# Weight narrowing handed out by single steps, four output banks in turn, and loads issued by need, in a fused retention and two-layer expert kernel

## The chip, the core and the metric

The kernel runs on one core of one Trainium2 chip. The metric is device time in microseconds of one execution, taken as the median of several. Engines are named as in the profile: PE (matmul), DVE, ACT, POOL and SP, which only issues DMAs.

## What is computed

```python
def _attn_ref(q, k, v):                      # B=4, H=8, S=768, D=64
    for t in range(S):                       # one decay rate gamma per head
        state = gamma * state + outer(k[:, :, t], v[:, :, t])
        y[:, :, t] = scale * q[:, :, t] @ state
    return y
...
x = attn_out as (3072 tokens, 512)
h = x @ moe_w_in                             # 512 -> 2048
g = where(h > 0, h, exp(min(h, 0)) - 1)
x = g @ moe_w_out                            # 2048 -> 512
h = x @ moe2_w_in
P = a[0] + a[1]*h + a[2]*h**2 + a[3]*h**3
Q = 1 + abs(b[0])*abs(h) + abs(b[1])*h**2
return (P / (Q + 1e-06)) @ moe2_w_out
```

## The kernel before

**Precision and weights.** The inputs are in float64. The big products are done as three fp32r matmuls each (high*high, high*low, low*high). Each of the four weight matrices is cut into 16 tiles, `wi` for the first product and `wo` for the second. A tile comes in as 512 KB of pairs of 32-bit words into one of three staging buffers `st` (`load_w`, L87), and is made into fp32 by one ACT instruction (`narrow_a`, L97, "the abs" below) and four DVE instructions (`narrow_b`, L110, L111, L112, L114, "the four steps"). Then `split_w` cuts it into a high part (ACT, L123) and a low part (POOL, L124). The list `todo` gives the order: weight 0 is `wi` tile 0, weight 1 is `wo` tile 0, weight 2 is `wi` tile 1, and so on; the first 32 belong to the first layer. Those of the second layer are narrowed later and stored to DRAM (`w2s`).

**Order.** Instructions of one engine run in the order in which the code writes them; engines wait for each other by semaphores alone. A DMA waits in SP's queue until its buffer is free, and all later DMAs of SP wait behind it.

**Up-front passes.** The sequence of 768 is cut into chunks of 128 tokens, six to a batch entry. Ten passes i = 0 to 9 do chunks 0 to 4, half of the heads in each pass (c = i // 2, g = i % 2). A pass does the scores (`sc`, L254), the chunk's addition to the state (`so`, L242 with the old state times a diagonal of decays `diag`, and L244), the masked scores `A` on DVE (L266), and, one pass later, the output (`at_out`: L275 and L278 into the same bank as `so`). Then ACT copies the state (L293) and the high part `xh` (L306), and DVE makes the low part `xl` (L307). Which of the PSUM banks `so` lies in is set in `at_in`. Weights 0 to 5 are narrowed in some of the passes: two steps behind `A`, two behind `xl`. Chunks are loaded in these passes too (`load_q`, `load_k`, 1 MB a chunk), and `scale_q`, `scale_k` on POOL multiply them by decays.

**Inner tiles.** After the passes one loop runs over (token block j, tile f) in the order of `seq`: six tiles of block 0, all 16 of block 1, the last ten of block 0, then blocks 2 to 5. An inner tile is: 12 matmuls of the first product (g1, into `h`), Relu and Exp on ACT (L598, L599), L603 on DVE, `gh` on ACT (L606), `gl` on POOL (L607), and 12 matmuls of the second product (g2, into the four banks `acc`), which are issued one tile later. In the first six tiles a further attention pass lies between g1 and g2 (`attn_a`, `attn_b`). `quota` says how many whole weights a tile narrows (0, 1 or 2): three steps before the Relu, the fourth behind L603, the split behind it, then the four steps of a second weight, and at the end the abs of the next.

```python
        run(steps[0:3])
...
        steps[3]()
...
        d1()
        run(steps[4:8])
        d2()
        if quota[it] and nabs[0] < nload[0]:
            abs_next()
```

After the first layer's last block the second layer runs over all blocks with weights that are ready.

Of the kernel before, what the change touches and what calls it, by code (L numbers as in the profile page):

```python
# [49 lines left out]
def retention_ffn_kernel(ctx: ExitStack, tc: tile.TileContext, qkT, kv, w1i, w1o, w2i, w2o, a_, b_, tab, out):  # L50
# [169 lines left out]
    def at_in(i, early=False):  # L220
# [7 lines left out]
        if early and i % 2:  # L228
# [236 lines left out]
    load_k(2)  # L465
    load_q(3)
    load_k(3)
    load_w(0, 0, 1)
# [17 lines left out]
    nc.gpsimd.tensor_copy(eye[:, 0:1], tri_t[:, 0:1])  # L486
    nc.gpsimd.tensor_tensor(out=eye[:, 1:C], in0=tri_t[:, 1:C], in1=tri_t[:, 0:C - 1], op=ALU.subtract)
    for p in range(NP):
        nc.gpsimd.tensor_scalar_mul(diag[:, p, :], eye, gc_t[:, p:p + 1])
# [29 lines left out]
    for i in range(10):  # L519
# [5 lines left out]
        at_mask(i, True)  # L525
        run(ops[0:2])
        if i:
            at_out(i - 1)
            run(at_state(i - 1))
            at_x(i - 1)  # L530
            if g == 0:
                load_q(c + 3)
                load_k(c + 3)
        run(ops[2:4])
        if ops:
            done()
            load_next()
            ops = []
        if i in (2, 4, 5, 6, 7, 8):
            ops, done = conv_next()  # L540
        if i == 9:
            abs_next()
# [3 lines left out]
    load_q(8)  # L546
    load_k(8)
    load_kr(2 * LATE)
    qp = atw.tile([128, 2, NP, C], F32R, tag="k0", name="qp", bufs=1)
    for e in range(2):  # L550
        nc.gpsimd.memset(qp[64 - 64 * e:128 - 64 * e, e].bitcast(F32), 0.0)
# [8 lines left out]

    half0 = 6
    seq = [(0, f) for f in range(half0)] + [(1, f) for f in range(KF)] + [(0, f) for f in range(half0, KF)]
    seq += [(j, f) for j in range(2, NB) for f in range(KF)]
    quota = [1, 1, 1, 2, 1, 2] + [1, 2, 1, 1, 2, 1, 1, 2] + [1] * 7 + [0] * 3 + [1] * 7 + [0]
    quota += [int(f % 2 == 1 or (j, f) == (2, 2)) for j in (2, 3, 4) for f in range(KF)] + [0] * KF
    assert sum(quota) == len(todo) - 6 and len(quota) == len(seq)
# [7 lines left out]
    for it, (j, f) in enumerate(seq):  # L574
# [7 lines left out]
        x1 = x2 = [none] * 4  # L582
        d1 = d2 = none
        if quota[it]:
            x1, d1 = conv_next()
        if quota[it] > 1:
            x2, d2 = conv_next()
        steps = x1 + x2
# [5 lines left out]
        run(steps[0:3])  # L594
# [4 lines left out]
        nc.scalar.activation(out=t, in_=t, func=ACTF.Exp, scale=-1.0)  # L599
        run(st)  # L600
# [7 lines left out]
        steps[3]()  # L608
        if it < half0 + 8:
            fill(3 if quota[it] < 2 else 2)  # L610
        else:
            fill(1)
        d1()
        run(steps[4:8])
        d2()
        if quota[it] and nabs[0] < nload[0]:
            abs_next()
# [16 lines left out]
        if it < half0 + 8:  # L634
            fill(3)
# [113 lines left out]
```

## Time and profile before

| what | value |
|---|---|
| median of 3 runs | 1204.96 us (1204.39 to 1205.35) |
| time of the profiled execution | 1204.38 us |
| its span, first to last instruction | 1202.6 us |
| PE busy in the span | 1181.9 us (98%) |
| DVE, ACT, POOL busy | 830.5, 689.8, 452.7 us |
| mean granted clock of PE | 0.996 |

The span is the stretch that the trace shows; some 1.8 us of the profiled execution's time lie around it. PE's busy time is 98% of the span, and the page's row of the 40 slices of PE falls below nine tenths in the first two slices and in the last alone. A matmul counts as busy from its issue to its modelled end.

### The profile page before, as it was taken

What the parts mean: (1) busy time and instruction counts of PE and PEld (TensorE: products, weight loads), DVE (VectorE), ACT (ScalarE), POOL (GpSimd) and SP (SyncE); (2) the same over time, 40 slices, a digit from 0 to 9 for tenths busy, and PEclk for the clock granted to TensorE, in tenths of its full rate; (3) what the DMA queues carried; (4) which work ended last, traced back from release to release, by engine and by line L of the source; (5) the groups of instructions that cost most, each with busy time, mean ns of one, the idle gap of its engine ahead of it and who ended that gap; (6) DMA issues with size and microseconds to landing.
All of it is one profiled execution on the core that took longest, in us unless ns stands there. A gap on an engine that the chain in (4) does not pass through costs nothing.

```text
span 1202.6 us, 15571 instructions
## 1 busy us (share of the span) xinstructions
PE 1181.9 (98%) x5684; PEld 993.6 (83%) x5684; DVE 830.5 (69%) x1228; ACT 689.8 (57%) x1214; POOL 452.7 (38%) x376
## 2 busy tenths in 40 slices
PE   8899999999999999999999999999999999999998
PEld 7787778888888888888888888888888888888887
DVE  4888775876666556665311598788888888888775
ACT  2445554444444444444455787777776767776765
POOL 6454554443333333322378533233223232232222
PEclk9999999999999999999999999999999999999999
DMA  9724331554224322422243300200100200200000
GB/s 260 222 86 153 107 111 68 171 171 167 88 88 141 126 89 91 151 89 75 88 123 107 113 10 1 62 10 1 62 10 1 70 1 1 70 1 1 35 1 35
DMA packets 57068, 97.81 MB, mean 81 GB/s; under 512 B 11680, under 2 KB 25120, under 8 KB 56992
## 3 DMA queue, kind: packets, MB, share of 16 engines
q1 hardware_dynamic: 56704, 96.49, 25.1%
q8 instruction: 44, 0.72, 0.2%
q10 hardware_dynamic: 288, 0.34, 0.1%
q14 instruction: 32, 0.26, 0.1%
HBM read 74.79 MB, written 22.02 MB: 81 GB/s over the span
## 4 chain that ended last, share of the span: by engine, by line
PE 89%; DVE 6%; ACT 2%; issue 1%; DMA 1%; POOL 0%; ACTq 0%; DVEq 0%
PE acc L341 41%; PE h L341 40%; PE so L278 3%; PE sc L341 2%; DVE wc L112 1%; DVE wc L111 1%; DVE wc L110 1%; PE so L244 1%; PE so L275 1%; DVE wc L114 1%; ACT wc L97 1%; DMA qT<-in_qkT_dram 1%; DVE t L603 1%; DVE xl L307 0%; ACT gh L606 0%
## 5 line engine op out<-in xcount | busy, mean ns | idle before, releaser
L341 PE MATMUL h<-xh,wi 128*128 128x512 f32 x1536 | 507.1, 391 | 0.0
L341 PEld LDWEIGHTS h<-xh,wi 128*128 128x128 f32 x1536 | 288.4, 188 | 58.9
L341 PE MATMUL h<-xl,wi 128*128 128x512 f32 x768 | 299.2, 390 | 0.0
L678 POOL TENSOR_TENSOR gl<-e,gh 128x512 fp32r<-128x512 f32 x96 | 124.7, 1299 | 349.6 <-ACT gh L677 214.4
L607 POOL TENSOR_TENSOR gl<-t,gh 128x512 fp32r<-128x512 f32 x96 | 124.2, 1293 | 320.8 <-ACT gh L606 293.8
L341 PE MATMUL acc<-gh,wo 128*128 128x512 f32 x768 | 196.1, 398 | 6.3 <-ACT gh L606 4.9
L341 PE MATMUL acc<-wo,gh 128*128 128x512 f32 x768 | 190.1, 389 | 0.0
L341 PEld LDWEIGHTS acc<-gh,wo 128*128 128x128 f32 x768 | 142.2, 189 | 36.3 <-ACT gh L606 6.2
L341 PEld LDWEIGHTS acc<-wo,gh 128*128 128x128 f32 x768 | 144.1, 188 | 29.9
L341 PEld LDWEIGHTS h<-xl,wi 128*128 128x128 f32 x768 | 144.4, 188 | 29.0
L603 DVE SCALAR_TENSOR_TENSOR t<-t,h 128x512 f32<-128x512 f32 x96 | 65.6, 683 | 128.0 <-ACT t L599 127.9
L598 ACT ACTIVATE t<-h 128x512 f32<-128x512 f32 x96 | 57.2, 595 | 148.4 <-PE h L341 148.0
L652 ACT ACTIVATE s<-h 128x512 f32<-128x512 f32 x96 | 57.4, 598 | 137.8 <-PE h L341 137.8
L606 ACT CAST gh<-t 128x512 fp32r<-128x512 f32 x96 | 59.7, 622 | 108.9 <-DVE t L603 108.9
L658 DVE SCALAR_TENSOR_TENSOR u<-s,b,u 128x512 f32<-128x512 f32 x96 | 71.9, 749 | 56.4 <-ACT u L653 55.8
L341 PE MATMUL acc<-wo,gl 128*128 128x512 f32 x384 | 103.1, 389 | 0.0
L341 PE MATMUL acc<-gl,wo 128*128 128x512 f32 x384 | 103.1, 390 | 0.0
L668 DVE SCALAR_TENSOR_TENSOR e<-e,ab,r 128x512 f32<-128x512 f32 x96 | 72.2, 752 | 32.2 <-ACT r L662 32.2
L669 DVE SCALAR_TENSOR_TENSOR u<-u,r 128x512 f32<-128x512 f32 x96 | 87.6, 913 | 0.0
L341 PEld LDWEIGHTS acc<-gl,wo 128*128 128x128 f32 x384 | 72.1, 188 | 15.7
L341 PEld LDWEIGHTS acc<-wo,gl 128*128 128x128 f32 x384 | 72.1, 188 | 15.0
L654 ACT ACTIVATE e<-h,ab 128x512 f32<-128x512 f32 x96 | 74.9, 780 | 0.0
(107 smaller groups left out, 1609.5 us busy)
## 6 DMA issues: line engine op xcount, KB each, us to landing
st<-in_w1i_dram SPq DMA_DIRECT2D x16, 512.0 KB, 3.6
st<-in_w1o_dram SPq DMA_DIRECT2D x16, 512.0 KB, 3.5
st<-in_w2i_dram SPq DMA_DIRECT2D x16, 512.0 KB, 4.7
st<-in_w2o_dram SPq DMA_DIRECT2D x16, 512.0 KB, 3.7
w2s<-wc SPq DMA_DIRECT2D x32, 256.0 KB, 2.1
wc<-w2s SPq DMA_DIRECT2D x32, 256.0 KB, 2.7
xs<-y SPq DMA_DIRECT2D x24, 256.0 KB, 3.6
qT<-in_qkT_dram SPq DMA_DIRECT2D x20, 256.0 KB, 3.9
```

The costliest lines, as they stand in the source:

```text
L278: nc.tensor.matmul(out=so[:, p, :], lhsT=vw[:, 2 * g + p, e:e + 2, :], rhs=A[:, 2 * p + e, :], start=(c % CB == 0 and e == 0), stop=(e == 1))
L341: nc.tensor.matmul(out=ps, lhsT=lh, rhs=rh, start=first and idx == 0, stop=last and idx == len(pairs) - 1)
L598: nc.scalar.activation(out=t, in_=h, func=ACTF.Relu, scale=-1.0)
L603: nc.vector.scalar_tensor_tensor(out=t, in0=t, scalar=-1.0, in1=h, op0=ALU.add, op1=ALU.max)
L606: nc.scalar.copy(gh, t)
L607: nc.gpsimd.tensor_tensor(out=gl, in0=t, in1=gh.bitcast(F32), op=ALU.subtract)
L652: nc.scalar.activation(out=s, in_=ps, func=ACTF.Square)
L654: nc.scalar.activation(out=e, in_=ps, func=ACTF.Identity, scale=ab[:, 3:4], bias=ab[:, 2:3])
L658: nc.vector.scalar_tensor_tensor(out=u, in0=s, scalar=b1, in1=u, op0=ALU.mult, op1=ALU.add)
L668: nc.vector.scalar_tensor_tensor(out=e, in0=e, scalar=ab[:, 0:1], in1=r, op0=ALU.add, op1=ALU.mult)
L669: nc.vector.scalar_tensor_tensor(out=u, in0=u, scalar=QC, in1=r, op0=ALU.add, op1=ALU.mult)
L678: nc.gpsimd.tensor_tensor(out=gl, in0=e, in1=gh.bitcast(F32), op=ALU.subtract)
```

## The change

It joins five edits.

1. In the up-front passes `so` takes four banks in turn (`acc3`, two buffers of `h`, one of `pst`); before, every odd pass took `acc3`.
2. The diagonal of decays is made by DVE (six small instructions) and no longer by POOL.
3. In the passes the abs of the next weight stands before the split of the present one, and weights are narrowed in passes 3, 4, 5, 6, 8, 9 instead of 3, 5, 6, 7, 8, 9.
4. Loads are reordered: weight 1 before chunk 3; chunk 6 two passes later, chunk 7 behind the first inner tile, chunk 8 and the zeroing of `qp` behind the third.
5. In the inner tiles `nops` gives single steps (five in most tiles) instead of whole weights. Three stand before the Relu, the rest behind L603 (L624 in the changed kernel). The split of a weight whose four steps are done stands behind the next Relu and Exp (`finish`), in block 1; in the other blocks also at the end of the tile's DVE work. The abs runs at most one weight ahead.

```diff
--- before.py
+++ after.py
@@ -225,7 +225,7 @@
             sc = psa.tile([128, 4, C], F32, tag=f"acc{i % 4}", name="sc")
         else:
             sc = pst.tile([128, 4, C], F32, tag="sc", name="sc")
-        if early and i % 2:
+        if early and i % 4 == 1:
             so = psa.tile([128, 4, C], F32, tag="acc3", name="so")
         elif early and i % 4:
             so = psh.tile([128, 4, C], F32, tag="h", name="so")
@@ -463,9 +463,9 @@
     load_w(0, 0, 0)
     load_q(2)
     load_k(2)
+    load_w(0, 0, 1)
     load_q(3)
     load_k(3)
-    load_w(0, 0, 1)
     load_w(0, 1, 0)
     ab = const.tile([128, 6], F32, name="ab")
     nc.sync.dma_start(out=ab[:, 0:4], in_=a_.rearrange("(o n) -> o n", o=1).to_broadcast([128, 4]))
@@ -483,10 +483,14 @@
     scale_k(0)
     scale_q(1, nc.gpsimd)
     eye = dg[:, 512:512 + C]
-    nc.gpsimd.tensor_copy(eye[:, 0:1], tri_t[:, 0:1])
-    nc.gpsimd.tensor_tensor(out=eye[:, 1:C], in0=tri_t[:, 1:C], in1=tri_t[:, 0:C - 1], op=ALU.subtract)
-    for p in range(NP):
-        nc.gpsimd.tensor_scalar_mul(diag[:, p, :], eye, gc_t[:, p:p + 1])
+
+    def decay_diag(p):
+        nc.vector.tensor_scalar_mul(diag[:, p, :], eye, gc_t[:, p:p + 1])
+
+    nc.vector.tensor_copy(eye[:, 0:1], tri_t[:, 0:1])
+    nc.vector.tensor_tensor(out=eye[:, 1:C], in0=tri_t[:, 1:C], in1=tri_t[:, 0:C - 1], op=ALU.subtract)
+    decay_diag(0)
+    decay_diag(1)
     todo = [(ph, f, e) for ph in range(2) for f in range(KF) for e in range(2)]
     nload, nabs, nconv = [3], [0], [0]
 
@@ -523,32 +527,29 @@
             scale_k(c + 2)
         at_in(i, True)
         at_mask(i, True)
+        if i == 0:
+            decay_diag(2)
+            decay_diag(3)
         run(ops[0:2])
         if i:
             at_out(i - 1)
             run(at_state(i - 1))
             at_x(i - 1)
-            if g == 0:
-                load_q(c + 3)
-                load_k(c + 3)
+            if i in (2, 4, 8):
+                load_q(min(c + 3, 6))
+                load_k(min(c + 3, 6))
         run(ops[2:4])
+        if i in (3, 4, 5, 7, 8, 9):
+            abs_next()
         if ops:
             done()
             load_next()
             ops = []
-        if i in (2, 4, 5, 6, 7, 8):
+        if i in (2, 3, 4, 5, 7, 8):
             ops, done = conv_next()
-        if i == 9:
-            abs_next()
     at_out(9)
     run(at_state(9))
     at_x(9)
-    load_q(8)
-    load_k(8)
-    load_kr(2 * LATE)
-    qp = atw.tile([128, 2, NP, C], F32R, tag="k0", name="qp", bufs=1)
-    for e in range(2):
-        nc.gpsimd.memset(qp[64 - 64 * e:128 - 64 * e, e].bitcast(F32), 0.0)
     nc.scalar.activation(out=b1, in_=ab[:, 5:6], func=ACTF.Abs)
     nx[0] = 9
     attn_b()
@@ -558,12 +559,37 @@
         nc.sync.dma_start(out=c, in_=w2s[f][e])
         W[1, f, e, "c"] = c
 
+    qp = atw.tile([128, 2, NP, C], F32R, tag="k0", name="qp", bufs=1)
+    def first_late():
+
+        load_q(LATE)
+        load_k(LATE)
+        load_kr(2 * LATE)
+        for e in range(2):
+            nc.gpsimd.memset(qp[64 - 64 * e:128 - 64 * e, e].bitcast(F32), 0.0)
+
     half0 = 6
     seq = [(0, f) for f in range(half0)] + [(1, f) for f in range(KF)] + [(0, f) for f in range(half0, KF)]
     seq += [(j, f) for j in range(2, NB) for f in range(KF)]
-    quota = [1, 1, 1, 2, 1, 2] + [1, 2, 1, 1, 2, 1, 1, 2] + [1] * 7 + [0] * 3 + [1] * 7 + [0]
-    quota += [int(f % 2 == 1 or (j, f) == (2, 2)) for j in (2, 3, 4) for f in range(KF)] + [0] * KF
-    assert sum(quota) == len(todo) - 6 and len(quota) == len(seq)
+    nops = [5, 5, 5, 5, 6, 6] + [5] * 12 + [4] * 3 + [0] * 3 + [4] * 7 + [0]
+    nops += [4 * int(f % 2 == 1 or (j, f) == (2, 2)) for j in (2, 3, 4) for f in range(KF)] + [0] * KF
+    assert sum(nops) == 4 * (len(todo) - 6) and len(nops) == len(seq)
+    stream, ends = [], []
+
+    def narrow(n):
+
+        for _ in range(n):
+            if not stream:
+                ops, done = conv_next()
+                stream.extend(ops)
+                ends.append([done])
+            stream.pop(0)()
+            if not stream:
+                ends[-1].append(True)
+
+    def finish():
+        while ends and len(ends[0]) > 1:
+            ends.pop(0)[0]()
 
     def fill(n):
 
@@ -579,24 +605,19 @@
         at_b = both or (1 < j < NB - 1 and f % 2 == 1)
         h = psh.tile([128, 512], F32, tag="h", name="h")
         g1(h, f, xh, xl)
-        x1 = x2 = [none] * 4
-        d1 = d2 = none
-        if quota[it]:
-            x1, d1 = conv_next()
-        if quota[it] > 1:
-            x2, d2 = conv_next()
-        steps = x1 + x2
+        n = nops[it]
         st = []
         if at_a:
             low = prep(nx[0] + 1)
             at_mask(nx[0])
             low()
-        run(steps[0:3])
+        narrow(min(n, 3))
         if at_a:
             st = attn_a()
         t = tmp("t", "t")
         nc.scalar.activation(out=t, in_=h, func=ACTF.Relu, scale=-1.0)
         nc.scalar.activation(out=t, in_=t, func=ACTF.Exp, scale=-1.0)
+        finish()
         run(st)
         if at_a:
             at_x(nx[0])
@@ -605,16 +626,16 @@
         gl = gp.tile([128, 512], F32R, tag="gl", name="gl")
         nc.scalar.copy(gh, t)
         nc.gpsimd.tensor_tensor(out=gl, in0=t, in1=gh.bitcast(F32), op=ALU.subtract)
-        steps[3]()
-        if it < half0 + 8:
-            fill(3 if quota[it] < 2 else 2)
+        if j == 1:
+            if n and nabs[0] < min(nload[0], nconv[0] + 1):
+                abs_next()
+            narrow(max(n - 3, 0))
         else:
-            fill(1)
-        d1()
-        run(steps[4:8])
-        d2()
-        if quota[it] and nabs[0] < nload[0]:
-            abs_next()
+            narrow(max(n - 3, 0))
+            if n and nabs[0] < min(nload[0], nconv[0] + 1):
+                abs_next()
+            finish()
+        fill((3 if it < half0 + 8 else 1) - (1 if stream else 0))
         if last:
             split_w(1, f, 0)
             if f + 1 < KF:
@@ -632,9 +653,14 @@
                 split_w(1, f - 1, 1)
             load_c(f, 1)
         if it < half0 + 8:
-            fill(3)
+            fill(2 if stream else 3)
         elif not last and it not in (19, 20, 21, 30, 31, 47, 63, 79):
             fill(2)
+        if it == 0:
+            load_q(7)
+            load_k(7)
+        if it == 2:
+            first_late()
         if (j, f) == (0, KF - 1):
             load_ya()
         if j == NB - 2 and f == KF - 1:
```

What the change moves on the engines is shown at three places. The first is ACT in passes 2 to 4 (`St` is the state, `xh` the high part of the block's input, L97 the abs, L123 the split). Before:

```order
L306 CAST xh<-so 128x2x128
L123 CAST wi_324<-wc 128x512
L293 COPY St<-so 64x2x64 x2
L306 CAST xh<-so 128x2x128
L97 ACTIVATE wc<-st 128x512
L293 COPY St<-so 64x2x64 x2
L306 CAST xh<-so 128x2x128
L123 CAST wo_387<-wc 128x512
L97 ACTIVATE wc<-st 128x512
```

and changed:

```order
L306 CAST xh<-so 128x2x128
L97 ACTIVATE wc<-st 128x512
L123 CAST wi_326<-wc 128x512
L293 COPY St<-so 64x2x64 x2
L306 CAST xh<-so 128x2x128
L97 ACTIVATE wc<-st 128x512
L123 CAST wo_366<-wc 128x512
L293 COPY St<-so 64x2x64 x2
L306 CAST xh<-so 128x2x128
L97 ACTIVATE wc<-st 128x512
```

Each pass has an abs now, and the abs stands ahead of the split, which waits for DVE's fourth step. An abs that waits for its load holds the copies of the state behind it.

The second is SP's queue behind chunk 5 (rows of `v_139`), with the loads of weights 4 to 7 (L87) and of chunk 6 (`li_145` to `lo_154`). Before:

```order
L172 DMA v_139<-in_kv_dram 128x3x128
L173 DMA v_139<-in_kv_dram 128x2x64
L87 DMA st<-in_w1i_dram 128x1024
L158 DMA li_145<-in_qkT_dram 128x512
L163 DMA li_145<-in_kv_dram 128x512
L167 DMA li_156<-in_qkT_dram 64x512 x2
L172 DMA lo_154<-in_kv_dram 128x3x128
L173 DMA lo_154<-in_kv_dram 128x2x64
L87 DMA st<-in_w1o_dram 128x1024
L87 DMA st<-in_w1i_dram 128x1024
L158 DMA lo_146<-in_qkT_dram 128x512
```

and changed:

```order
L172 DMA v_139<-in_kv_dram 128x3x128
L173 DMA v_139<-in_kv_dram 128x2x64
L87 DMA st<-in_w1i_dram 128x1024
L87 DMA st<-in_w1o_dram 128x1024
L87 DMA st<-in_w1i_dram 128x1024
L158 DMA li_145<-in_qkT_dram 128x512
L163 DMA li_145<-in_kv_dram 128x512
L167 DMA li_156<-in_qkT_dram 64x512 x2
L172 DMA lo_154<-in_kv_dram 128x3x128
L173 DMA lo_154<-in_kv_dram 128x2x64
L87 DMA st<-in_w1o_dram 128x1024
L87 DMA st<-in_w1i_dram 128x1024
```

Weights 4, 5 and 6 follow chunk 5 one behind the other; before, chunk 6 stood between weights 4 and 5.

The third is DVE in three tiles of block 1 (L603 and L624 are the same instruction of an inner tile). Before, one weight, one weight and the first of two:

```order
L603 SCALAR_TENSOR_TENSOR t<-t,h 128x512
L114 SCALAR_TENSOR_TENSOR wc<-st,wc 128x512
L110 TENSOR_SCALAR wc<-wc 128x512
L111 TENSOR_SCALAR wc<-wc 128x512
L112 SCALAR_TENSOR_TENSOR wc<-st,wc 128x512
L114 SCALAR_TENSOR_TENSOR wc<-st,wc 128x512
L110 TENSOR_SCALAR wc<-wc 128x512
L111 TENSOR_SCALAR wc<-wc 128x512
L112 SCALAR_TENSOR_TENSOR wc<-st,wc 128x512
```

and changed:

```order
L624 SCALAR_TENSOR_TENSOR t<-t,h 128x512
L110 TENSOR_SCALAR wc<-wc 128x512
L111 TENSOR_SCALAR wc<-wc 128x512
L112 SCALAR_TENSOR_TENSOR wc<-st,wc 128x512
L114 SCALAR_TENSOR_TENSOR wc<-st,wc 128x512
L110 TENSOR_SCALAR wc<-wc 128x512
L624 SCALAR_TENSOR_TENSOR t<-t,h 128x512
L111 TENSOR_SCALAR wc<-wc 128x512
L112 SCALAR_TENSOR_TENSOR wc<-st,wc 128x512
L114 SCALAR_TENSOR_TENSOR wc<-st,wc 128x512
L110 TENSOR_SCALAR wc<-wc 128x512
L111 TENSOR_SCALAR wc<-wc 128x512
L624 SCALAR_TENSOR_TENSOR t<-t,h 128x512
```

Between one L603 and the next stood four or eight steps; now five stand there, and a weight's four steps lie across the boundary of tiles.

## Rows read from the trace of the kernel before

**Rows 1.** Stages (us): busy time (instructions) of PE, PEld, DVE, ACT, POOL; PE clock; DMA share, GB/s

```profile
6.40:48.94 42.54, 35.50 (x272) 34.29 (x273) 27.56 (x48) 14.22 (x38) 21.19 (x21) 0.92 0.94 267
48.94:103.08 54.14, 52.18 (x298) 45.14 (x296) 42.71 (x56) 27.99 (x59) 29.73 (x24) 1.00 0.35 116
103.08:166.43 63.35, 57.01 (x241) 45.75 (x240) 50.88 (x67) 34.01 (x59) 31.25 (x23) 0.97 0.37 129
166.43:1203.00 1036.57, 1032.32 (x4867) 864.91 (x4865) 706.53 (x1050) 612.26 (x1058) 365.68 (x295) 1.00 0.21 68
```

**Rows 2.** Waits of PE from 0 to 166 us: total us, times, longest us

```profile
PE acc L341 <- ACT gh L606: 4.9, 3, 2.5
PE so L242 <- DVE xl L307: 4.2, 3, 1.9
PE so L244 <- POOL lo L183: 2.1, 1, 2.1
PE so L278 <- DVE A L266: 2.0, 3, 1.1
...
PE acc L341 <- ACT li L398: 1.4, 1, 1.4
```

**Rows 3.** Timeline of DVE, end of the passes: start, duration, instruction, idle before it

```profile
40.64 0.69 DVE L114 SCALAR_TENSOR_TENSOR wc<-st,wc 128x512 int32<-128x512 int32 x1
...
46.98 1.03 DVE L110 TENSOR_SCALAR wc<-wc 128x512 f32<-128x512 f32 x1 [0.66 <-ACT wc L97]
...
49.44 0.69 DVE L114 SCALAR_TENSOR_TENSOR wc<-st,wc 128x512 int32<-128x512 int32 x1
...
52.53 0.68 DVE L266 TENSOR_TENSOR A<-sc,mask 128x512 f32<-128x512 f32 x1
53.13 2.68 DVE L110 TENSOR_SCALAR wc<-wc 128x512 f32<-128x512 f32 x1
55.84 0.43 DVE L111 TENSOR_SCALAR wc<-wc 128x512 int32<-128x512 int32 x1
```

**Rows 4.** Timeline of ACT at the end of the passes

```profile
50.16 0.62 ACT L123 CAST wo<-wc 128x512 fp32r<-128x512 f32 x1 [2.20 <-DVE wc L114]
50.69 0.66 ACT L97 ACTIVATE wc<-st 128x512 f32<-128x512 f32 x1
51.25 0.52 ACT L293 COPY St<-so 64x128 f32<-64x128 f32 x2
```

**Rows 5.** Timeline of SP's queue: issue of weight 3's load and chunk 5's last

```profile
25.52 0.41 SPq L87 DMA_DIRECT2D st<-in_w1o_dram  x1
...
29.80 0.43 SPq L173 DMA_DIRECT2D v<-in_kv_dram  x1
```

**Rows 6.** DMA issues in 25.5:25.6 and 29.79:29.83 us: KB, us from issue to landing

```profile
st<-in_w1o_dram SPq DMA_DIRECT2D x1, 512.0 KB, 5.4
...
v<-in_kv_dram SPq DMA_DIRECT2D x1, 64.0 KB, 4.8
```

**Rows 7.** Chain that ended last, from 160 us: start, us, what

```profile
169.31 2.72 PE acc L341 x12
172.03 2.72 PE h L341 x12
```

**Rows 8.** Timeline of PE: the longest wait in block 1

```profile
139.01 1.22 PE L341 MATMUL acc<-gh,wo 128*128 128x512 f32 x2 [2.49 <-ACT gh L606]
```

**Rows 9.** Groups of DVE instructions, 103:166 us: count, busy us, mean ns, idle before

```profile
L111 DVE TENSOR_SCALAR wc<-wc 128x512 int32<-128x512 int32 x14 | 15.7, 1120 | 0.5
L112 DVE SCALAR_TENSOR_TENSOR wc<-st,wc 128x512 int32<-128x512 int32 x13 | 11.9, 916 | 0.4
L110 DVE TENSOR_SCALAR wc<-wc 128x512 f32<-128x512 f32 x14 | 9.0, 643 | 12.6 <-ACT wc L97 12.6
L114 DVE SCALAR_TENSOR_TENSOR wc<-st,wc 128x512 int32<-128x512 int32 x13 | 8.9, 686 | 0.1
L603 DVE SCALAR_TENSOR_TENSOR t<-t,h 128x512 f32<-128x512 f32 x10 | 6.8, 681 | 0.0
```

**Rows 10.** Timeline of POOL and DVE in block 1

```profile
126.32 1.48 POOL L124 TENSOR_TENSOR wi<-wc,wi 128x512 fp32r<-128x512 f32 x1
...
126.69 1.40 DVE L111 TENSOR_SCALAR wc<-wc 128x512 int32<-128x512 int32 x1
```

**Rows 11.** Timeline of SP's queue in block 1: two loads that share a buffer

```profile
110.91 0.33 SPq L87 DMA_DIRECT2D st<-in_w1i_dram  x1
...
124.95 0.33 SPq L87 DMA_DIRECT2D st<-in_w1o_dram  x1
```

## The prediction

> **What bounds the kernel now.** I read the table of stages first [rows 1]. The reader is to see that from 166.43 us to the end PE is busy for 1032.32 of 1036.57 us, at full clock; what is missing lies behind the last matmul. Nothing that the change does there can matter as long as it adds no wait: the order on all engines is the same as before from the end of block 1 on. In the three stages ahead of it PE is idle for 42.54 - 35.50 = 7.0, 54.14 - 52.18 = 2.0 and 63.35 - 57.01 = 6.3 us, and in the first and third its clock is below full (0.92 and 0.97). So the whole change is about some 20 us at the start.
>
> The second view is the waits of PE in that stretch [rows 2]: 4.9 us for `gh` and 1.4 us for copies of the accumulators in block 1, 4.2 us for `xl`, which holds the bank that the next odd pass wants, 2.1 us for the scaled chunk 1, 2.0 us for `A`. Behind all of them stands the narrowing of weights. In the passes DVE's last step of a weight starts every 4.40 us (at 40.64 and 49.44, with one between) [rows 3], while PE could do a pass in less; in block 1 tiles with two weights make L603 late, then `gh`, then g2, by up to 2.49 us [rows 8].
>
> How long block 1 must take follows from the chain of work further on: 12 matmuls take 2.72 us, a tile 2 x 2.72 = 5.44 us [rows 7]. Ten tiles lie between 103.08 and 166.43, 54.4 us of work in 63.35 us: **8.95 us are lost there**, 6.3 in waits and the rest at a lower clock behind them (the clock of the stage is 0.97).
>
> **Block 1: single steps.** The same number of steps is done over the stage; what is new is how they lie. DVE's need per tile: as measured, with everything that holds them up inside their durations, the four steps take 0.643 + 1.120 + 0.916 + 0.686 = 3.37 us a weight, L603 0.68 [rows 9]. Five steps and one L603 make 1.25 x 3.37 + 0.68 = 4.89 us, less than PE's 5.44. A tile of two weights needed 7.4, and the waits for the abs came on top: 12.6 us in 14 weights, since it stood behind `gh` and the split [rows 9]. Now the abs runs a weight ahead in three tiles of four, and the split stands behind Exp. ACT per tile has Relu, Exp, `gh` and 1.25 of split and abs, some 3.4 us at the 0.6 or so that each takes [rows 4], so neither engine is full. `gh` is wanted by PE a whole tile, 5.44 us, after its `h` is done. I take all 8.95 us as won; the lower bound is worked out with the rivals.
>
> One row speaks against it. L111 takes 1.40 us when it meets a running POOL subtraction and 0.43 us otherwise, and it ends 0.29 us behind POOL's end (126.69 + 1.40 against 126.32 + 1.48) [rows 3, 10]. The Trainium skill ("SBUF — State Buffer", "Who interferes with whom") says the same as a rule: DVE and GpSimd share a port pair, and a DVE instruction in a 2-port mode or with two SBUF inputs waits for the whole of a GpSimd one. It speaks against this change, because a DVE that no longer idles behind the abs starts more of its steps while POOL runs. By that rule alone, with every step held that meets POOL, up to the 6.3 us of the first rival below would be given back.
>
> By the rows of before the holds cost 3.37 - 2.23 = 1.14 us a weight, where 2.23 is two steps at 0.43 and two at 0.69 (L110 unheld taken as long as L111). DVE keeps pace with PE up to (5.44 - 0.68) / 1.25 = 3.81 us a weight, that is holds of 1.58 us.
>
> **The passes.** Each of the removed waits (2.1 for chunk 1, behind the diagonal on POOL; 4.2 for `xl`, through the fourth bank) is hidden by what is late next: first the loads, then the narrowing. DMA moves 267 GB/s through the stage at a share of 0.94 [rows 1], so loads come no sooner. Weight 3's load stands in the same place of the stream as before and lands at 25.52 + 5.4 = 30.9 us [rows 5, 6]; its abs (0.66) ends at 31.6. In pass 6 its four steps (2.23) and `xl` (0.4), with one hold of about 1.0, end at 35.2; before, weight 3 ended at 40.64 + 0.69 = 41.3. That is 6.1 us ahead, because pass 4 has a weight now. Weight 4 follows chunk 5, which lands at 29.80 + 4.8 = 34.6; 512 KB at 267 GB/s are 2.0 us, so it lands at 36.6 and its abs ends at 37.2. Two weights follow at 4.40 - 0.66 = 3.74 us each (the abs no longer stands behind the split), 44.7, and with one further hold about 45.7; before, weight 5 ended at 50.13. What follows is a fixed chain: split, abs, state, `xh`, `xl`, then `A` of the tenth pass at 52.53, for which PE waits [rows 3, 4]; the abs leaves it (51.25 - 50.69 = 0.56 us). So the first inner tile gets its `A` 4.4 + 0.56 = 5.0 us sooner, with one hold fewer 6.0. I take 5.5. Bounds: 2.1 us if the last two weights take 4.40 + 1.0 us each (no wait saved, one hold more): 37.2 + 10.8 = 48.0 against 50.13. 10 us if narrowing holds nothing and PE goes by the landing of chunk 5: 34.6, a scaling on POOL of 1.5 as the subtraction takes [rows 10], some 30 small matmuls at 35.50 / 272 = 0.13 us [rows 1] and the first g1 of 2.72 us [rows 7] come to 42.7 against 52.53. A loss in this stage would need weight 3 to be narrowed later than before, and its load, which sets it, stands where it stood.
>
> The diagonal on DVE costs six instructions of 128 columns or fewer, below 1 us in all, at a place where DVE waits for the first scores; I cost it at nothing, and 1 us if POOL's scaling of chunk 0 holds it.
>
> **The six tiles of block 0.** They lose 2.0 us to waits now. The zeroing of `qp` no longer stands in front of L110 (2.68 us at 53.13 instead of 0.43 [rows 3]), but a fifth step, with an inline abs in front of it, now stands between L603 and the next `A`, and PE waits for `A`. With tiles of about 7.7 us DVE has room, apart from the first two. I take 0, between -1.5 and +1.5. Chunks 7 and 8 come later, but one to two tiles ahead of their scaling.
>
> **The sum.** 5.5 + 0 + 8.9 = 14.4 us off the profiled execution's 1204.4 gives **1190.0 us**. The profiled execution is 0.6 us below the median shown, so no correction is made.
>
> **Rivals.**
> - *POOL's holds fill DVE in block 1.* For: the row on L111 and the loss of the idle time that kept them apart. Against: 1.14 is well below 1.58. At 2.0 us of holds a weight, 4.23 us, a tile takes 1.25 x 4.23 + 0.68 = 5.97; 0.53 us over twelve tiles with five steps are 6.3 of the 8.9 given back: 1196.3.
> - *The passes stay where they were.* Every abs now stands ahead of the split and of the copies of the state, and DMA is full; a late landing holds ACT, hence the state, hence PE. Then only block 1 pays, with 2 us at most from the passes: about 1194.5.
> - *The passes open up to PE's own pace.* If fewer holds occur than I count, the stage ends 8 to 10 us sooner, and the tiles of block 0 lose nothing: 10 + 1 + 8.9, 1184.5.
> - *Slower: the three staging buffers become the bound of block 1.* Now a buffer comes round in 124.95 - 110.91 = 14.0 us [rows 11], paced by DVE. At 1.25 weights a tile it must come round in 3 x 5.44 / 1.25 = 13.1. Abs and steps have their slots once a tile, so a load that misses a slot costs up to 5.44 us. At 17.2 us a tile would take 17.2 / 3 x 1.25 = 7.17, 1.73 more than PE needs, 20.8 us over twelve tiles: 1204.4 + 20.8 - 8.9 - 5.5 = 1210.8. It decides for slower from about 16.4 us on (16.8 us lost). Against it: a load lands in some 5 us [rows 6], and the load is asked for behind the fourth step of the weight three places ahead, so that by my count of slots four microseconds or more are left.
>
> **How the numbers follow.** A measurement of this kernel tells about 0.2%, 2.4 us, from no change. Chances: my forecast 0.55, the holds 0.13, the passes unchanged 0.12, the passes opened 0.13, the staging buffers 0.04, and 0.03 for gains and losses that cancel. The range reaches from the opened passes (1184.5) to just beyond the holds with a little less from the passes as well (1197.0); the slower rival and a part of the unlikeliest mixtures are left out. Faster by over 0.2%: 0.93; within: 0.03; slower: 0.04.
>
> **What would show it.** In the profile after, PE's waits for `gh` in block 1 should be gone, and ten tiles there take 54 to 55 us at a clock of 1.00; L110 should no longer wait for L97 except for one tile in four. The waits of L242 for `xl` should be gone, and in their place PE waits for the state (L293) or for `A` in passes 6 to 9, while L97 waits for loads of weights 2 to 4. `A` of the tenth pass should start at about 47 us. From the end of block 1 on, the timeline should be the same, shifted. I am wrong if L111, L112 and L110 together take over 3.1 us a weight in block 1, if ACT waits for loads there, or if a new wait shows up behind 150 us.

## The result and the profile after

The changed kernel takes **1191.79 us** (median of four, 1190.54 to 1192.73) against 1205.15 (1204.39 to 1205.66) for the kernel before: a ratio of 0.9889, 95% interval 0.9872 to 0.9906. The forecast was 1190.0 in a range of 1184.5 to 1197.0. The profiled execution shown below, 1192.73 us, is the slowest of the four.

The stages of the changed kernel, cut at the same events as [rows 1] (columns as there):

```profile
6.75:46.11 39.36, 33.92 (x273) 32.81 (x273) 28.76 (x54) 14.71 (x39) 20.34 (x15) 0.96 0.95 270
46.11:100.01 53.90, 51.76 (x297) 44.97 (x296) 43.24 (x60) 28.30 (x59) 30.95 (x24) 1.00 0.41 134
100.01:154.43 54.42, 54.42 (x242) 45.06 (x241) 49.02 (x62) 33.26 (x58) 30.50 (x22) 1.00 0.39 135
154.43:1191.00 1036.57, 1032.59 (x4867) 864.82 (x4865) 711.22 (x1051) 612.43 (x1059) 367.97 (x296) 1.00 0.21 69
```

PE's waits in the whole execution, which answer to [rows 2]:

```profile
PE so L242 <- ACT St L293: 4.3, 2, 2.5
PE so L278 <- DVE A L266: 2.1, 2, 1.5
PE wps L477 <- DVE warm L434: 1.5, 1, 1.5
PE so L244 <- POOL n L183: 0.6, 1, 0.6
PE sc L254 <- POOL li L178: 0.4, 1, 0.4
```

In block 1 PE is busy for all of 54.42 us, at full clock, and no wait for `gh` is left; the last wait of PE in the whole execution ends before 57 us. From the end of the ten tiles to the last instruction the kernel takes 1036.5 us, before 1036.1. Measured from the first score matmul to the first g1, and from g1 to g1, the stages changed like this (the third stage of the views begins with the second tile of block 1, so its first tile is counted with block 0):

| us | before | after | saved |
|---|---|---|---|
| up-front passes | 42.50 | 39.30 | 3.20 |
| six tiles of block 0, first of block 1 | 54.13 | 53.90 | 0.23 |
| next ten tiles of block 1 | 63.35 | 54.40 | 8.95 |
| ahead of the first score and behind the ten tiles | 1042.59 | 1043.35 | -0.76 |

Block 1 gave all that was forecast, to the hundredth. In this execution the passes gave 3.2 where 5.5 were forecast. The DVE instructions from 100 to 155 us, answering to [rows 9]:

```profile
L114 DVE SCALAR_TENSOR_TENSOR wc<-st,wc 128x512 int32<-128x512 int32 x13 | 12.3, 950 | 0.3
L111 DVE TENSOR_SCALAR wc<-wc 128x512 int32<-128x512 int32 x13 | 11.6, 889 | 0.3
L112 DVE SCALAR_TENSOR_TENSOR wc<-st,wc 128x512 int32<-128x512 int32 x12 | 11.4, 950 | 0.3
L110 DVE TENSOR_SCALAR wc<-wc 128x512 f32<-128x512 f32 x13 | 10.5, 804 | 4.4 <-ACT wc L97 4.4
L624 DVE SCALAR_TENSOR_TENSOR t<-t,h 128x512 f32<-128x512 f32 x10 | 6.8, 680 | 0.0
```

The four steps take 0.950 + 0.889 + 0.950 + 0.804 = 3.59 us a weight, 1.36 of it holds (1.14 before). The holds did grow, as the row on L111 had warned, but stayed under the 1.58 at which DVE was to fall behind. The wait for the abs fell from 12.6 to 4.4 us, and that is nearly all of DVE's idle time: in the ten tiles DVE stood idle for 63.35 - 50.88 = 12.5 us before and 54.42 - 49.02 = 5.4 now.

The end of the passes on DVE, answering to [rows 3]: the last steps of weights 3, 4 and 5 (L114), the `xl` that stands in front of weight 4's last two steps, and the `A` for which PE waits:

```profile
34.92 0.69 DVE L114 SCALAR_TENSOR_TENSOR wc<-st,wc 128x512 int32<-128x512 int32 x1
...
41.67 0.42 DVE L307 TENSOR_TENSOR xl<-so,xh 128x256 fp32r<-128x256 f32 x1 [1.37 <-ACT xh L306]
42.02 0.68 DVE L112 SCALAR_TENSOR_TENSOR wc<-st,wc 128x512 int32<-128x512 int32 x1
42.73 0.69 DVE L114 SCALAR_TENSOR_TENSOR wc<-st,wc 128x512 int32<-128x512 int32 x1
...
46.74 0.69 DVE L114 SCALAR_TENSOR_TENSOR wc<-st,wc 128x512 int32<-128x512 int32 x1
...
49.27 0.68 DVE L266 TENSOR_TENSOR A<-sc,mask 128x512 f32<-128x512 f32 x1
```

And on ACT, where the abs (L97) of weight 3 (at 31.64) and of weight 4 (at 38.35) stand:

```profile
31.64 0.66 ACT L97 ACTIVATE wc<-st 128x512 f32<-128x512 f32 x1 [3.87 <-POOL n L183]
...
37.51 0.54 ACT L293 COPY St<-so 64x128 f32<-64x128 f32 x2 [1.25 <-PE so L278]
38.08 0.37 ACT L306 CAST xh<-so 128x256 fp32r<-128x256 f32 x1
38.35 0.69 ACT L97 ACTIVATE wc<-st 128x512 f32<-128x512 f32 x1
```

POOL's L183 was over long before 31.64; that abs waited for its load, which by its DMA record landed at 31.55. Weight 3 ended at 34.92 + 0.69 = 35.61 (35.2 forecast). Weight 4's load landed at 37.17, but its abs ended at 39.04 (37.2 forecast): the copies of the state and `xh` stand in front of it on ACT and waited for PE's L278. Then weight 4 took until 43.42 and weight 5 until 47.43, so 4.38 and 4.01 us. Together that is 8.39 us where 7.48, or 8.48 with one hold, were forecast: two of a weight's steps stand behind `xl`, which waits for `xh`, so a weight cannot be quicker than a pass. The first inner tile's `A` came at 49.27, 3.26 us sooner than in [rows 3], not 5.5.

### The profile page after: what moved, and what is told of

Its sections match the earlier page's. It is cut to its first block, busy times and chain, and to the rows that moved or that the text cites. A ratio compares the mean times of both kernels' runs of the same rounds, so it can differ in the third digit from the quotient of the medians.

```text
span 1190.9 us, 15583 instructions
## 1 busy us (share of the span) xinstructions
PE 1177.9 (99%) x5684; PEld 991.5 (83%) x5684; DVE 835.0 (70%) x1234; ACT 690.0 (58%) x1214; POOL 454.6 (38%) x370
## 4 chain that ended last, share of the span: by engine, by line
PE 93%; DVE 2%; DMA 2%; POOL 1%; issue 1%; ACT 1%; SPq 0%; POOLq 0%; ACTq 0%; DVEq 0%
PE acc L341 43%; PE h L341 42%; PE so L278 3%; PE sc L341 2%; PE so L244 1%; PE so L275 1%; DMA lo<-in_qkT_dram 1%; DMA st<-in_w1i_dram 0%; DMA k<-in_qkT_dram 0%; POOL gl L628 0%; PE sc L254 0%; DVE wc L112 0%; POOL wi L124 0%; DVE wc L111 0%; DVE wc L110 0%
## 5 line engine op out<-in xcount | busy, mean ns | idle before, releaser
L628 POOL TENSOR_TENSOR gl<-t,gh 128x512 fp32r<-128x512 f32 x96 | 128.9, 1343 | 274.2 <-ACT gh L627 266.2
L624 DVE SCALAR_TENSOR_TENSOR t<-t,h 128x512 f32<-128x512 f32 x96 | 65.5, 682 | 128.8 <-ACT t L619 128.8
L694 DVE SCALAR_TENSOR_TENSOR e<-e,ab,r 128x512 f32<-128x512 f32 x96 | 72.1, 752 | 32.5 <-ACT r L688 32.5
L112 DVE SCALAR_TENSOR_TENSOR wc<-st,wc 128x512 int32<-128x512 int32 x64 | 73.7, 1151 | 1.8
```

The costliest lines, as they stand in the source:

```text
L112: lambda: v.scalar_tensor_tensor(out=ci, in0=t[:, :, 1], scalar=-0x40000000, in1=ci, op0=ALU.bitwise_and, op1=ALU.bitwise_or),
L624: nc.vector.scalar_tensor_tensor(out=t, in0=t, scalar=-1.0, in1=h, op0=ALU.add, op1=ALU.max)
L628: nc.gpsimd.tensor_tensor(out=gl, in0=t, in1=gh.bitcast(F32), op=ALU.subtract)
L694: nc.vector.scalar_tensor_tensor(out=e, in0=e, scalar=ab[:, 0:1], in1=r, op0=ALU.add, op1=ALU.mult)
```

## The experiments

My theory: block 1 is worth 8.9 us and belongs to edit 5, the single steps, alone; the passes are worth some 3 to 5 us and end with narrowing and loads. Rivals: POOL's holds fill DVE as soon as it stops idling; parts of the change do nothing; the clock or the place of the abs explains what the passes missed.

**The two halves apart.** First the steps alone, edit 5, on the kernel before:

```diff
-    quota = [1, 1, 1, 2, 1, 2] + [1, 2, 1, 1, 2, 1, 1, 2] + [1] * 7 + [0] * 3 + [1] * 7 + [0]
+    nops = [5, 5, 5, 5, 6, 6] + [5] * 12 + [4] * 3 + [0] * 3 + [4] * 7 + [0]
...
-        run(steps[0:3])
+        narrow(min(n, 3))
```

> The kernel before with edit 5 alone (single steps in the inner tiles, abs ahead, split behind Exp). Theory: block 1 pays by itself, 8.9 us: about 1196.2 us, ten tiles of block 1 in 54.4 us, the passes as before (42.5 us). Rival: single steps only keep pace because the passes hand over weights earlier; then waits for gh stay in block 1 and the time is 1200 us or more.

Measured 1199.66 us (1196.68 to 1201.10), ratio 0.9954 (0.9941 to 0.9966). Its passes, block 0 and block 1:

```profile
6.76:51.62 44.86, 35.75 (x272) 34.39 (x273) 26.44 (x47) 14.21 (x38) 20.71 (x21) 0.92 0.94 261
51.62:106.44 54.82, 51.76 (x298) 44.98 (x296) 43.34 (x60) 28.83 (x60) 30.57 (x24) 1.00 0.35 111
106.44:160.84 54.40, 54.40 (x242) 45.05 (x240) 48.99 (x62) 33.28 (x58) 30.50 (x22) 1.00 0.41 136
```

Block 1 takes 54.40 us with this edit alone, and no wait for `gh` is left, so the rival fell. The 3.5 us that are missing to the expectation lie ahead of it: the passes took 2.4 us more than in [rows 1] with the same instructions in the same order, and loads landed later in them (by the DMA records weight 0 at 16.11 us against 15.11, weight 5 at 42.81 against 41.55), and a tile of block 0 waited 2.3 us for `A`. Only the fastest of its five executions came near the 1196.2.

Then everything but the steps, edits 1 to 4:

```diff
-    nops = [5, 5, 5, 5, 6, 6] + [5] * 12 + [4] * 3 + [0] * 3 + [4] * 7 + [0]
+    quota = [1, 1, 1, 2, 1, 2] + [1, 2, 1, 1, 2, 1, 1, 2] + [1] * 7 + [0] * 3 + [1] * 7 + [0]
```

> The changed kernel with the inner tiles' whole weights of before (edits 1 to 4 alone). Theory: the passes gain their 3.3 us and block 1 loses its 9 us as before: about 1201.8 us. Rival: what the passes gain is waited for again in block 0 or block 1, as the same weights are wanted there: 1205 us, no change from before.

Measured 1199.74 us (1198.64 to 1202.42), ratio 0.9963 (0.9949 to 0.9976). PE's waits, the first two rows:

```profile
PE acc L341 <- ACT gh L616: 4.7, 3, 2.5
PE so L242 <- ACT St L293: 4.6, 3, 2.3
```

Block 1 is that of before (63.39 us, 4.7 us of waits for `gh`); the passes take 38.93 and block 0 52.85. The time is 2.1 us below the expectation; block 0, for which I had counted nothing, gave 1.3. So edit 5 owns block 1 and the other edits what is ahead of it. Edit 5 itself joins three things, the single steps, the abs ahead of its weight and the split behind Exp, and no run takes these apart; the fall of the waits for the abs, 8.2 us, is nearly as large as the whole gain in block 1. In the medians of that comparison (1204.93 us before) the halves are worth 5.3 and 5.2 us, 2.9 less than the whole change; in size that is what the steps alone lost ahead of block 1 in their trace (2.4 in the passes, 0.7 in block 0), and why those loads landed later is open.

**Edits undone one at a time.** One output bank less (edit 1):

```diff
-        if early and i % 4 == 1:
+        if early and i % 2:
```

> The changed kernel with edit 1 undone (odd passes share the bank acc3 again). Theory: the state product of passes 5, 7 and 9 waits for xl of two passes before, which ends 0.8 us behind the point where it starts now in each; half of that reaches the end of the passes: 1193 us. Rival A: it waits for the state anyway, 1191.8 us. Rival B: all of the 4.2 us of before come back, 1196 us.

Measured 1194.79 us (1193.96 to 1195.23), ratio 0.9916 (0.9902 to 0.9929). The first row of PE's waits:

```profile
PE so L242 <- DVE xl L307: 6.8, 4, 2.9
```

The waits for `xl` are back, and all four executions lie above all four of the changed kernel: 3 us by the medians, between my theory (1193) and rival B (1196). Rival A fell. The two intervals of the ratio just overlap.

The old loads (edit 4):

```diff
-            if i in (2, 4, 8):
-                load_q(min(c + 3, 6))
+            if g == 0:
+                load_q(c + 3)
...
-        if it == 2:
-            first_late()
```

> The changed kernel with edit 4 undone (weight 1 behind chunk 3, chunks 6 and 7 in the passes, chunk 8 and the zeroing of qp behind them). Theory: weight 1 lands 3 us later and weight 5 some 4 us later (42.6 us, behind chunk 6), which is about when its abs is due; 1 to 2 us on the passes and up to 1 us on the first inner tile: 1194 us. Rival A: loads are not what holds the passes, 1191.8 us. Rival B: they are all of the gain of the passes, 1195 us or more.

Measured 1195.46 us (1194.95 to 1198.29), ratio 0.9927 (0.9915 to 0.9940). Its first two rows of PE's waits:

```profile
PE so L242 <- ACT St L293: 4.8, 3, 3.4
PE so L278 <- DVE A L266: 3.3, 2, 2.6
```

This interval lies clear of the changed kernel's. In its trace the passes took 40.31 us, 1.0 more, and block 0 55.05, 1.2 more, since its second tile waits 2.6 us for `A`. The time is that of rival B; rival A, that loads do not matter, fell.

The old place of the abs and the old six passes with a weight (edit 3):

```diff
-        if i in (3, 4, 5, 7, 8, 9):
-            abs_next()
...
-        if i in (2, 3, 4, 5, 7, 8):
+        if i in (2, 4, 5, 6, 7, 8):
```

> The changed kernel with edit 3 undone (abs behind the split of the weight before it, weights in passes 3, 5, 6, 7, 8, 9). Theory: a weight takes 4.4 us again from pass 5 on and none is done in pass 4, so the passes lose about what they won: 1195 us, with DVE waiting for the abs in every pass. Rival: the loads pace the passes and the place of the abs hardly matters: 1192 us.

Measured 1192.67 us (1192.03 to 1193.16), ratio 0.9886 (0.9872 to 0.9901): no difference from the changed kernel that these runs can tell, so my theory fell and the rival held. By its trace weight 3 now ends at 38.55 us, three later, but weight 5 at 47.35, as in the changed kernel, and the passes take 39.31. Getting weight 3 done early, from which I had counted the gain, shows no worth by itself.

The decay's diagonal on POOL again (edit 2):

```diff
-    nc.vector.tensor_copy(eye[:, 0:1], tri_t[:, 0:1])
+    nc.gpsimd.tensor_copy(eye[:, 0:1], tri_t[:, 0:1])
...
-        nc.vector.tensor_scalar_mul(diag[:, p, :], eye, gc_t[:, p:p + 1])
+        nc.gpsimd.tensor_scalar_mul(diag[:, p, :], eye, gc_t[:, p:p + 1])
```

> The changed kernel with the decay's diagonal built on POOL again (edit 2 undone). In the kernel before, that building took 2.94 us on POOL ahead of the scaling of chunk 1, and PE waited 2.1 us for that scaling in the second pass. My theory is that this wait is hidden by what is late next, the loads: PE waits some 2 us for L183 again, later passes still wait for their chunks and for weight 3 as they land, so the passes stay at 38.5 to 40 us and the kernel at 1191.5 to 1192.5. Rival: the 2.1 us are on the path and come back whole, passes of 41.4 us, 1194.

Measured 1194.85 us (1193.19 to 1194.89), ratio 0.9903 (0.9886 to 0.9919). The wait is back, and the stage with it:

```profile
PE so L244 <- POOL lo L183: 2.0, 1, 2.0
```

```profile
6.41:48.24 41.83, 35.70 (x273) 34.35 (x273) 27.67 (x47) 14.90 (x39) 21.37 (x21) 0.92 0.89 254
```

My theory most likely fell here: the passes took 41.83 us, 2.5 more, and all four executions lie above all four of the changed kernel. The wait of 2.1 us in the second pass was not hidden by what is late next. Of the 2.5 us only 0.7 are more idle time of PE; 1.8 are longer busy time (35.70 us against 33.92). Behind the wait, which ends at 14.69 us, PE has the lower of its two clock levels (0.50) for 3.4 us, as in the kernel before (15.64 to 19.06 us) and not in the changed kernel:

```profile
15.67:19.09 3.42, 3.42 (x18) 3.42 (x17) 0.60 (x2) 1.46 (x4) 2.26 (x2) 0.50 1.08 320
```

(The two intervals of the ratio overlap, so the size of the loss, 1.7 us by the ratios and 3.1 by the medians, is not settled.)

**What the passes missed.** Three attempts to win the rest. Matmuls on zeros, whose results are overwritten, ahead of the state's products in passes 6 and 7, so that PE keeps its clock (the stage's granted clock is 0.96; in the changed kernel PE waits 2.48 us for the state at 33.30 us, and the clock from 33.0 to 37.5 us is 0.62):

```diff
+        if early and i in WARM:
+            for _ in range(WARM[i]):
+                nc.tensor.matmul(out=so, lhsT=warm[:, 0:128], rhs=warm, start=True, stop=True)
         kv_sum()
```

> The changed kernel with 7 and 10 matmuls of zeros into the bank so ahead of the state products of passes 6 and 7, where PE waits 1.8 and 2.5 us for the state; they are overwritten by the real products, and nothing is left out. Theory: the low clock behind the wait costs about 1.7 us (the twelve groups from 33.30 to 37.26 us take 3.96 us instead of 2.25) and lies on the path to weight 4's abs, so the time falls to about 1190.3 us and PE's clock in the passes is 1.00. Rival A: the clock is beside the path, 1191.8 us. Rival B: the added matmuls outlast the wait and push the state product back: 1192.5 us or more.

Measured 1192.59 us (1191.57 to 1193.55), ratio 0.9888 (0.9871 to 0.9905). The passes, beside those of the changed kernel above:

```profile
6.68:44.99 38.31, 36.19 (x289) 34.05 (x290) 31.21 (x53) 14.83 (x39) 19.72 (x15) 1.00 1.00 275
```

The clock is full and the waits for the state are gone, but the time is not better; rivals A (1191.8) and B (1192.5 or more) both lie within its four executions. Then the loads of weights 3 to 5 ahead of chunks 4 and 5:

```diff
-            if i in (2, 4, 8):
-                load_q(min(c + 3, 6))
+            if i == 8:
+                load_q(6)
...
+            if i in (3, 5):
+                load_q((i + 5) // 2)
```

> The changed kernel with weight 3's load ahead of chunk 4 and those of weights 4 and 5 ahead of chunk 5. Theory: weight 3's abs waits for its load now (landed 31.55 us, ACT idle 3.9 us) and holds the state behind it; landed at about 28.5 us it takes 3 us off the passes: 1189 us, with A of the tenth pass at about 46.5 us. Rival: chunk 4 and 5 land 2 to 4 us later and PE or POOL waits for them instead: 1191.8 us or more.

Measured 1191.88 us (1190.71 to 1193.44), ratio 0.9881 (0.9866 to 0.9896). By the DMA records weight 3 landed at 28.44 us instead of 31.55, and the first `A` of the tiles came at 47.18, 2.1 sooner than in the changed kernel's trace, yet the median shows no gain. Chunks 4 and 5 landed 2.7 us later, as the rival had it. And four steps in the first inner tile, where an abs and a fifth step stood between L624 and the next `A`:

```diff
-    nops = [5, 5, 5, 5, 6, 6] + [5] * 12 + [4] * 3 + [0] * 3 + [4] * 7 + [0]
+    nops = [4, 5, 5, 6, 6, 6] + [5] * 12 + [4] * 3 + [0] * 3 + [4] * 7 + [0]
```

> The changed kernel with four steps in the first inner tile and six in the fourth (4, 5, 5, 6, 6, 6 instead of 5, 5, 5, 5, 6, 6). Theory: the fifth step of the first tile and its abs stand in front of A of the eleventh pass, for which PE waits 1.5 us; without it the second tile takes 8.4 us instead of 9.93: 1190.3 us. Rival: the wait only moves to a later tile of block 0: 1191.8 us.

Measured 1192.39 us (1190.75 to 1193.36), ratio 0.9883 (0.9868 to 0.9898). In its trace the second tile takes 8.24 us instead of 9.93 and the third 8.44 instead of 7.70, so block 0 gives back 0.9 us (53.00 against 53.90); its passes, the same program as in the changed kernel, took 41.18 us, 1.9 more. The two together:

> The earlier loads of weights 3 to 5 and four steps in the first inner tile together. In their own profiled executions the first took the passes from 39.30 to 37.81 us, the second the first A-bound tile from 9.93 to 8.24. If both are gains of their own: 1188.5 to 1189.5. Rival (both are within what executions differ by through the landing of loads): 1191 to 1192.

Measured 1190.43 us (1189.41 to 1190.84), ratio 0.9872 (0.9858 to 0.9885), the fastest kernel of the study: passes 37.92, block 0 52.99, block 1 54.40. That is 1.4 us below the changed kernel's median; the intervals overlap, so it is likely, not certain, to be a gain.

What stays open is how much of each belongs to the kernel and how much to the execution. Five of these kernels have the same up-front passes, and their profiled executions took 37.86, 38.34, 38.93, 39.30 and 41.18 us there: one program, 3.3 us apart. Two with the passes of before took 42.50 and 44.87. The traces narrow it down. From the end of weight 4's abs to the first g1 it is 7.06 to 7.08 us in four of the five and 7.54 in the longest, so the passes differ in when that abs ends: at 37.70 us in the shortest, 39.04 in the changed kernel, 39.95 in the longest. In all five its load had landed 0.2 to 2.3 us before it began, so it is not that load which sets it. In the changed kernel and in the longest PE has its lower clock level (0.50) for a stretch ahead of that abs; in the other three the clock is full from 32.5 to 39.3 us:

```profile
33.51:36.92 3.41, 3.41 (x17) 3.41 (x17) 2.51 (x4) 0.75 (x2) 1.41 (x2) 0.50 1.06 325
32.48:39.31 6.83, 5.60 (x26) 5.60 (x27) 3.37 (x6) 2.97 (x10) 3.96 (x3) 0.50 0.90 284
```

Both stretches go with PE's longest waits for the state (2.48 and 3.70 us, which end at 33.30 and 33.71); in the other three traces these stay at 2.3 us or less. That the clock makes the difference is not shown: with the clock kept full the median was no better.

**POOL's holds, the rival of block 1.** A subtraction of 512 columns more on POOL in each of the first twelve tiles of block 1:

```diff
         nc.gpsimd.tensor_tensor(out=gl, in0=t, in1=gh.bitcast(F32), op=ALU.subtract)
+        if j == 1 and f < 12:
+            nc.gpsimd.tensor_tensor(out=kf.rearrange("p n a t -> p (n a t)"), in0=mask[:, 0:4, :].rearrange("p h t -> p (h t)"), in1=mask[:, 4:8, :].rearrange("p h t -> p (h t)"), op=ALU.subtract)
```

> One subtraction of 512 columns on POOL (two SBUF inputs, some 1.3 us by L124's 1299 ns) is added behind gl in the first twelve tiles of block 1; its result goes to an idle tile and is used by nobody. In the changed kernel DVE is busy for 49.02 of 54.42 us in block 1, so 0.54 us a tile are free; POOL is busy for 3.05 us a tile and DVE's steps are held for 1.70 us a tile. If the holds follow POOL's busy time, 1.28 us more of it add some 0.7 us of holds a tile (holds of 1.9 us a weight, above the 1.58 of the prediction): DVE needs 5.6 us a tile, ten tiles 55.5 to 57 us with PE waiting for gh (L627), 1194. If each such operation holds DVE for all of its length: 6.2 us a tile, ten tiles 61, about 1200. Rival (POOL and DVE do not hold each other any more than this, the free time takes it): ten tiles 54.4, L110, L111, L112 and L114 together at 3.6 us a weight, 1192.

Measured 1203.14 us (1201.40 to 1206.77), ratio 0.9982 (0.9973 to 0.9991). The groups on DVE from 100 to 161 us, then PE's first wait:

```profile
L112 DVE SCALAR_TENSOR_TENSOR wc<-st,wc 128x512 int32<-128x512 int32 x12 | 16.3, 1355 | 0.3
L111 DVE TENSOR_SCALAR wc<-wc 128x512 int32<-128x512 int32 x12 | 14.0, 1165 | 0.3
L114 DVE SCALAR_TENSOR_TENSOR wc<-st,wc 128x512 int32<-128x512 int32 x11 | 11.5, 1045 | 0.3
L110 DVE TENSOR_SCALAR wc<-wc 128x512 f32<-128x512 f32 x12 | 9.8, 818 | 5.7 <-ACT wc L97 5.7
```

```profile
PE acc L341 <- ACT gh L627: 7.6, 9, 1.4
```

One subtraction a tile, off the path and used by nobody, gives back 8.53 of the 8.95 us in ten tiles (62.93 us), beyond the far end of what I had expected (61 us, about 1200). The steps take 4.38 us a weight, 2.15 of it holds, above 1.58, and PE waits for `gh` nine times, six of them in the ten tiles. The rival of the prediction is a real mechanism that the changed kernel only just stays clear of.

The same time on POOL, but spent on writing zeros:

```diff
+            for n_ in (512, 512, 256):
+                nc.gpsimd.memset(kf.bitcast(F32).rearrange("p n a t -> p (n a t)")[:, 0:n_], 0.0)
```

> In place of that subtraction POOL writes zeros (512, 512 and 256 columns, some 1.29 us by the 517 ns of such a write) in the same tiles: as long on POOL, but with no input. If only POOL's reads hold the steps with two SBUF inputs (L112, L114) and its writes hold only L110 and L111, fewer steps are held: L112 and L114 stay at 950 ns, L110 and L111 grow, ten tiles 54.4 to 55.5 us, 1192 to 1193. If every operation of POOL holds every step alike, the time is that of the added subtraction.

Measured 1196.68 us (1196.35 to 1198.97), ratio 0.9928 (0.9916 to 0.9941), ten tiles 58.69 us. POOL (first two rows) and DVE around one tile:

```profile
118.51 1.64 POOL L631 MEMSET kf<- 128x512 f32 x3
120.12 1.46 POOL L124 TENSOR_TENSOR wi<-wc,wi 128x512 fp32r<-128x512 f32 x1
```

```profile
119.04 0.86 DVE L110 TENSOR_SCALAR wc<-wc 128x512 f32<-128x512 f32 x1
119.94 0.49 DVE L111 TENSOR_SCALAR wc<-wc 128x512 int32<-128x512 int32 x1
120.47 1.66 DVE L112 SCALAR_TENSOR_TENSOR wc<-st,wc 128x512 int32<-128x512 int32 x1
...
126.28 0.69 DVE L112 SCALAR_TENSOR_TENSOR wc<-st,wc 128x512 int32<-128x512 int32 x1
```

The L112 at 120.47 begins under a subtraction of POOL and takes 1.66; the one at 126.28 begins under a write of zeros (POOL's next three run from 124.69 to 126.50) and takes 0.69, as long as with no POOL at all. Of the L112 and L114 in the ten tiles that began under such a write, all ten took 0.69; of those that began under a subtraction, all ten took 1.19 to 1.67. L110 and L111 are held by writes too (0.86 and 0.49 above, 0.42 and 0.43 otherwise). The Trainium skill ("SBUF — State Buffer", "Who interferes with whom") says just this: a DVE instruction with two SBUF inputs contends with a GpSimd instruction that reads SBUF, not with one that only writes it; the trace agrees. In the prediction I gave the rule without that limit. The hold goes the other way as well: the subtractions that began at 126.46 and 150.70, each 0.2 us behind an L112, took 1.65 us where others take 1.30. But my expectation for the time was wrong. L112 and L114 went up all the same (to 1.14 and 1.04 from 100 to 155 us): ten of them now began under one of POOL's other subtractions, eight in the changed kernel, so the writes most likely pushed these on to meet them. The 1.72 us of holds a weight were again above 1.58.

## Why the prediction was right

**What bounds the kernel, and block 1.** Right in its steps, but for the size of DVE's need. The ten tiles take 54.40 us at full clock, L110 waits for the abs four times instead of ten, and nothing new waits behind 150 us. The runs agree with a limit of 1.58 us of holds, though they do not fix it: 1.36 leaves PE no wait, 1.72 and 2.15 do. What I missed is how close it is. I left DVE's own wait for the abs out of its need. Busy time and that wait come to 49.02 + 4.4 = 53.4 of 54.42 us in the changed kernel; with the added subtraction to 56.24 + 5.7 = 61.9 of 62.93, with the writes to 51.98 + 5.7 = 57.7 of 58.69. The 1.0 us that remain are the same in all three, also where PE waits for DVE, so they are the short gaps between instructions and no reserve. By that count nothing was left, not the half microsecond a tile that 4.89 against 5.44 promised, nor the 0.54 from which I expected the added subtraction to cost less. How much of the wait for the abs would give way to work is open; under load it grew to 5.7 us.

**The passes.** The direction and the waits were right: L242 waits for the state in place of `xl`, L97 waits for loads, weight 3 ends at 35.61. The term that was mis-sized is the abs of weight 4. I let it end at 37.2, as soon as its load had landed; it ended at 39.04. 0.6 us of that are the landing (37.17 against 36.6), some 1.2 the copies of the state that stand in front of it on ACT. "Two weights follow at 3.74 us each" was too quick as well, but the hold that I allowed beside it covered that: 8.39 us against 7.48 to 8.48. So the stage gave 3.2 us in that execution instead of 5.5. Over all executions the term may be larger: 13.4 us of difference in the medians less 8.95 and 0.2 leaves 4.2, and 4.9 if the 0.76 us lost outside these stages belong to every execution. Also, "Each of the removed waits is hidden by what is late next" was most likely wrong for the 2.1 us of chunk 1, as the diagonal on POOL showed; and the gain that I derived from weight 3 alone does not show, as the old place of the abs showed. That the passes still gained what lies between my bounds (2.1 to 10) is in part luck: one source of the gain that I counted on shows nothing, and one that I had called hidden most likely gave some.

**Block 0.** Forecast 0, measured 0.23, with the trade that was named: no L110 held for 2.68 us any more, but PE waits 1.47 us for `A` in the second tile, behind an abs and a fifth step. Four steps there take that back, with 0.74 us lost in the next tile.

**The slower rival.** The staging buffers never became the bound: no wait of L97 for a load shows in block 1.

## What to carry to other kernels

Work handed out in whole items can cost more than its sum: the same four steps a weight, dealt out five to a tile, with the abs a weight ahead and the split later, were worth 8.95 us in ten tiles; which of the three did it is not shown. Count the helper engine's need with its waits and with what other engines hold it up, and then test the margin by adding work to the engine that holds it: here one idle subtraction a tile took nearly all of the gain back. Judge a change in a stage that is bound by loads by several executions, since one program's profiles can lie 3 us apart there.

## What was not expected of the hardware

The same stretch of program, run by five kernels, took 37.86 to 41.18 us with the DMA engines busy at a share of 0.90 to 0.98. With the kernel before and the steps alone, whose passes hold the same instructions in the same order, loads landed 1.0 to 1.9 us apart. What decides when they land was not found. And in the run that added writes, a write of zeros on POOL held none of the ten L112 and L114, which have two SBUF inputs, that began under it, while a subtraction on POOL held all ten that began under one. The time grew by 4.9 us all the same.
